# Which rows of the wq gradient go out in which transfer: five three-way splits become two two-way splits, and the last group's stores become whole

## The chip, the cores and the metric

The kernel runs on one core of one Trainium2 chip. The metric is device time in microseconds of one execution; the time before is the median of three, 730.28 us (729.32 to 732.16). The profile is one execution of the same program, taken by the hardware profiler. Engines are named as the profile names them: PE (matrix multiply), DVE (vector), ACT (scalar), POOL (GpSimd) and SP (SyncE, which here only starts transfers). Transfers move on 16 DMA engines which all queues share; the profile gives their mean busy share, and the packet records of the trace give every packet's start, duration, size and queue, but not the number of the DMA engine it ran on.

## The reference: what is computed

One decode token (x of 640 values, bfloat16) goes through a layer norm; beside the residual there are two branches, attention over a cache of 8192 keys for 32 heads of 128, and a gated MLP of width 1728. The kernel returns the forward output and the gradients of all inputs but the MLP's unused one:

```python
xn = _layernorm(x, axis=-1)
return x + _A_ref(xn, A_k_cache, A_v_cache, A_wq, A_wo) + _B_ref(xn, B_w1, B_w3, B_w2)
...
_out, _vjp = jax.vjp(_f, A_x, A_k_cache, A_v_cache, A_wq, A_wo, B_w1, B_w3, B_w2)
_grads = _vjp(grad_out)
```

For the time two things matter. Each of the 32 heads reads its keys and values (2 MB each) once, and writes a gradient of the same size for each: 4 times 2 MB in and out per head. And the gradients of wq (640 by 4096) and wo (4096 by 640) are outer products, 5.2 MB each, written over the weights in SBUF and stored from there.

## The kernel before, in words

**Heads.** `head(h)` (L745) transposes K and V of one head on PE, forms scores, softmax and the backward pass, and `outer` (L464) writes the gradients over K and V in place on DVE. `store` (L477) sends a gradient out and calls `load_next` (L122), which loads the next K or V into a freed slot; there are ten slots of 2 MB, and `lag` keeps at least three of them free before the next load goes out. All of these transfers go through `fifo` (L104), that is through SP's queue, in the order V store, load, K store, load. Every one has 128 rows (partitions) of 16 KB.

**Groups.** Four heads make a group, g from 0 to 7. `load_group` (L109) brings 512 columns of wq as a tile of 128 rows by 5 by 512 (`wq_g`, 640 KB: five pieces of 1 KB in each row) and the matching rows of wo (`wo_g`, 640 KB: four pieces of 1,280 bytes in each row). Three buffers of each rotate. After a group's heads, during the next group, `fin_wo(g)` (L517) overwrites `wo_g` with its gradient and `fin_wq(g, ci)` (L523), called for ci from 0 to 4 at five places of the heads (L683 to L714), does the same to `wq_g`; both end in `store_group` (L505). After the last piece of wq, `fin_wq` also loads group g + 3 on POOL's queue.

**What `store_group` does before.** `fin_wq` calls it with `split` true for groups 1 to 5. Then the tile goes out in three transfers: rows 0 to 4 and rows 5 to 125 on POOL's queue, rows 126 and 127 on SP's. The wo gradients, and wq of groups 0 and 6, go out whole on POOL's queue. Group 7 is finished after all heads (L835 to L839), and each of its two gradients goes out in two transfers on SP's queue, rows 0 to 59 and rows 60 to 127.

**The end.** After group 7, DVE, PE and ACT form the two short rows (L841 to L867); ACT starts four small stores of them (L849, L867). SP and ACT take the semaphores of their transfers from one ring of eight in turn, so a transfer waits until the one eight places earlier in that ring has landed, besides its own data.

Of the kernel before, what the change touches and what calls it, by code (L numbers as in the profile page):

```python
# [16 lines left out]
P = 128  # L17
# [4 lines left out]
def kernel(  # L22
# [32 lines left out]
    NG = H // GH  # L55
    GW = GH * DH
# [23 lines left out]
    dwq_v = out_4.rearrange("(ci p) n -> p ci n", p=P)  # L80
# [23 lines left out]
    def fifo(out_, in_):  # L104
        nc.sync.dma_start(out_, in_)
# [3 lines left out]
    def load_group(g, eng):  # L109
        wq_g = wpool.tile([P, NC, GW], BF16, name="wq_g", tag="wq_g")  # L110
        eng.dma_start(wq_g[:], wq_v[:, :, g * GW:(g + 1) * GW])
        wo_g = wpool.tile([P, GH, D], BF16, name="wo_g", tag="wo_g")
        eng.dma_start(wo_g[:], wo_v[:, g * GH:(g + 1) * GH, :])
        grp[g] = dict(wq=wq_g, wo=wo_g)
# [389 lines left out]

    def store_group(g, dst, t, split=False):  # L505
        if split:
            for lo, hi in ((0, 5), (5, 126)):
                nc.gpsimd.dma_start(dst[lo:hi], t[lo:hi])
            fifo(dst[126:P], t[126:P])
            return  # L510
        if g < NG - 1:
            nc.gpsimd.dma_start(dst, t[:])
            return
        for lo, hi in ((0, 60), (60, P)):
            fifo(dst[lo:hi], t[lo:hi])

    def fin_wo(g):  # L517
        G_ = grp[g]
        for hh in range(GH):
            nc.vector.tensor_scalar(G_["wo"][:, hh, :], g_bc[:], G_["od"][:, hh, 0:1], None, ALU.mult)  # L520
        store_group(g, dwo_v[:, g * GH:(g + 1) * GH, :], G_["wo"])

    def fin_wq(g, ci):  # L523
        G_ = grp[g]
        wq_g, dqb = G_["wq"], G_["dqb"]
        nc.vector.scalar_tensor_tensor(wq_g[:, ci, :], wq_g[:, ci, :], 1.0, dqb, ALU.mult, ALU.mult,  # L526
                                       accum_out=dxa[:, ci, g:g + 1])
        nc.vector.tensor_scalar(wq_g[:, ci, :], dqb, xn_col[:, ci:ci + 1], None, ALU.mult)
        if ci == NC - 1:
            store_group(g, dwq_v[:, :, g * GW:(g + 1) * GW], wq_g, 1 <= g <= 5)  # L530
            grp.pop(g)
            if g + 3 < NG:
                load_group(g + 3, nc.gpsimd)
# [149 lines left out]
    def side_k(h):  # L683
        g, hh = divmod(h, GH)
        if hh == 1 and g > 0:
            fin_wq(g - 1, 0)
        elif hh == 2 and g > 0:
            fin_wq(g - 1, 3)
        elif hh == 3 and g + 1 < NG:
            prep_do(g + 1, 1)  # L690

    def side_m(h):
        g, hh = divmod(h, GH)
        if hh == 0 and g > 0:
            fin_od(g - 1)
        elif hh == 1 and g > 0:
            fin_wq(g - 1, 1)
        elif hh == 2 and g > 0:
            fin_wq(g - 1, 4)
        elif hh == 3 and g + 1 < NG:  # L700
            prep_do(g + 1, 2)
            prep_do(g + 1, 3)
# [195 lines left out]
```

## Time and profile before

| What | Value |
|---|---|
| median of three runs | 730.28 us (729.32, 730.28, 732.16) |
| profiled execution | span 727.5 us from the first to the last instruction; its time with what lies around the span is not given apart |
| PE, DVE, ACT, POOL busy | 83%, 63%, 52%, 4% of the span |
| read from and written to HBM | 151.34 MB each, 416 GB/s over the span |
| transfers on SP's queue (q1) | 22578 packets, 277.75 MB, 90.5% of 16 engines |
| transfers on POOL's queue (q0) | 5968 packets, 24.94 MB, 8.5% of 16 engines |

How to read it: the page cuts the span into 40 slices and gives busy shares in tenths; the row "DMA" is the mean over the 16 DMA engines. The table by stage gives the same share for any stretch. The list of SP's waits tells what ended each wait ahead of a transfer's start. A transfer's landing is counted by a semaphore that rises once for each DMA engine that took part, so the trace holds up to 16 landing times for each transfer, the first being the DMA engine that was furthest ahead and the last the one furthest behind.

### The profile page before, as it was taken

How to read it: one execution, taken by the hardware profiler on the slowest of the kernel's cores; microseconds unless marked ns; L12 is line 12 of the kernel's file. 1: busy time of each engine (PE TensorE's matmuls, PEld its weight loads, DVE VectorE, ACT ScalarE, POOL GpSimd, SP SyncE). 2: the span in 40 equal slices, each digit the busy share in tenths (PEclk: the TensorE clock that was granted, in tenths of full speed). 3: DMA queues.
4: the chain of work that ended last, by engine and by line, in shares of the span. 5: the costliest groups of instructions: out<-in, count | busy, mean ns of one | idle time of the engine just before them, and what ended most of it. 6: DMA issues, size and time to landing. Idle time of an engine off the chain costs nothing.

```text
span 727.5 us, 12942 instructions
## 1 busy us (share of the span) xinstructions
PE 603.3 (83%) x5186; PEld 377.1 (52%) x5193; DVE 459.8 (63%) x811; ACT 376.2 (52%) x727; POOL 32.3 (4%) x48
## 2 busy tenths in 40 slices
PE   4989489999899989888897789878796988988930
PEld 2547366665565556555454456445554555545510
DVE  4169646688868776667565756457665666667581
ACT  3640746665666566545454546455463555655510
POOL 0010100000000000000010000000000000000000
PEclk9997799999999999989998989899998999999965
DMA  9999999999999999999999999999999999999995
GB/s 351 400 411 421 428 426 430 427 426 430 420 420 431 430 412 420 426 428 421 420 425 428 430 426 428 420 431 428 421 422 427 429 425 423 425 432 427 426 415 221
DMA packets 28625, 303.54 MB, mean 417 GB/s; under 512 B 3354, under 2 KB 5929, under 8 KB 11924
## 3 DMA queue, kind: packets, MB, share of 16 engines
q1 hardware_dynamic: 22578, 277.75, 90.5%
q0 software_dynamic: 5968, 24.94, 8.5%
q8 instruction: 41, 0.67, 0.4%
q14 instruction: 20, 0.16, 0.1%
q10 hardware_dynamic: 18, 0.01, 0.0%
HBM read 151.34 MB, written 151.34 MB: 416 GB/s over the span
## 4 chain that ended last, share of the span: by engine, by line
DMA 51%; PE 36%; DVE 7%; ACT 2%; issue 1%; SPq 0%; ACTq 0%; DVEq 0%
DMA kv<-in_A_v_cache_dram 20%; PE pT L318 17%; DMA out_dram<-kv 16%; DMA kv<-in_A_k_cache_dram 14%; PE sA L339 5%; PE dA L339 4%; PE X L433 3%; DVE kv L466 3%; PE m L356 2%; DMA wo_g<-in_A_wo_dram 2%; ACT KT L320 1%; PE gu_ps L561 1%; PE pT L266 1%; PE m L400 1%; ACT KT L346 0%
## 5 line engine op out<-in xcount | busy, mean ns | idle before, releaser
L320 ACT COPY KT<-pT 128x512 f32<-128x512 f32 x512 | 288.3, 588 | 227.9 <-PE pT L318 208.6
L318 PE MATMUL pT<-ident_f,kv 128*128 128x128 f32 x2048 | 308.2, 290 | 53.7 <-DMA kv<-in_A_v_cache_dram 24.2
L318 PEld LDWEIGHTS pT<-ident_f,kv 128*128 128x128 f32 x2048 | 237.4, 149 | 146.2 <-PE pT L318 51.8
L466 DVE TENSOR_TENSOR kv<-qd,U 128x4096 bf16<-128x4096 bf16 x64 | 146.0, 2284 | 0.0
L466 DVE TENSOR_TENSOR kv<-qd,P 128x4096 bf16<-128x4096 bf16 x64 | 143.6, 2285 | 0.0
L433 PE MATMUL X<-kv,Z 128*32 128x512 bf16 x1024 | 97.1, 413 | 1.8 <-DVE Z L450 1.8
L339 PE MATMUL dA<-KT,qz 128*32 128x512 bf16 x512 | 84.2, 408 | 0.0
L339 PE MATMUL sA<-KT,qz 128*32 128x512 bf16 x512 | 83.5, 406 | 0.0
L416 DVE SCALAR_TENSOR_TENSOR U<-m,P 128x64 bf16<-128x64 f32 x32 | 7.5, 233 | 87.4 <-PE m L356 87.4
L433 PEld LDWEIGHTS <-Z 128*32 128x32 bf16 x1024 | 33.2, 101 | 35.3 <-issue 8.7
L339 PEld LDWEIGHTS <-qz 128*32 128x32 bf16 x1024 | 29.5, 95 | 40.8 <-issue 38.3
L382 DVE TENSOR_REDUCE mrow<-m 128x1 f32<-128x64 f32 x32 | 7.1, 223 | 68.4 <-PE m L356 68.3
L356 PE MATMUL m<-selc,KT 64*128 64x64 f32 x256 | 30.5, 242 | 10.3 <-ACT KT L346 10.3
L356 PEld LDWEIGHTS m<-selc,KT 64*128 64x128 f32 x256 | 21.5, 144 | 33.2 <-ACT KT L346 22.1
L376 ACT CAST qd<-pT 128x256 bf16<-128x256 f32 x32 | 11.9, 372 | 39.9 <-DVE kv L466 28.7
L389 DVE TENSOR_REDUCE negM<-m 128x1 f32<-128x128 f32 x32 | 9.3, 292 | 33.0 <-PE m L386 33.0
L526 DVE SCALAR_TENSOR_TENSOR wq_g<-wq_g,side 128x512 bf16<-128x512 bf16 x40 | 27.3, 683 | 0.0
L257 DVE SCALAR_TENSOR_TENSOR side<-wo_g,g_bc 128x640 bf16<-128x640 bf16 x32 | 26.2, 819 | 1.3 <-DMA wo_g<-in_A_wo_dram 0.9
L448 DVE SCALAR_TENSOR_TENSOR U<-m,P 128x128 bf16<-128x128 f32 x32 | 11.4, 356 | 16.3 <-PE m L446 16.3
L406 DVE RECIPROCAL rZ<-m 128x1 f32<-128x1 f32 x32 | 5.3, 166 | 24.2 <-PE m L400 24.2
L346 ACT COPY KT<-dA 64x512 f32<-64x512 f32 x32 | 18.6, 582 | 3.7 <-PE dA L339 3.7
L346 ACT COPY KT<-sA 64x512 f32<-64x512 f32 x32 | 18.6, 581 | 2.1 <-PE sA L339 1.9
(162 smaller groups left out, 372.7 us busy)
## 6 DMA issues: line engine op xcount, KB each, us to landing
out_dram<-kv SPq DMA_DIRECT2D x64, 2048.0 KB
kv<-in_A_k_cache_dram SPq DMA_DIRECT2D x32, 2048.0 KB
kv<-in_A_v_cache_dram SPq DMA_DIRECT2D x32, 2048.0 KB
wq_g<-in_A_wq_dram POOLq DMA_DIRECT2D x7, 640.0 KB, 13.4
wo_g<-in_A_wo_dram POOLq DMA_DIRECT2D x7, 640.0 KB, 19.1
out_dram<-wo_g POOLq DMA_DIRECT2D x7, 640.0 KB, 14.4
kv<-in_B_w_dram SPq DMA_DIRECT2D x2, 1728.0 KB
out_dram<-kv POOLq DMA_DIRECT2D x2, 1728.0 KB, 23.5
```

The source lines that it names most:

```text
L257: nc.vector.scalar_tensor_tensor(junk[:], G_["wo"][:, hh, :], 1.0, g_bc[:], ALU.mult, ALU.mult, accum_out=G_["do"][:, hh:hh + 1])
L318: nc.tensor.transpose(pT[:, k * P:(k + 1) * P], W3[:, 4 * c + k, :], ident_f[:])
L320: nc.scalar.copy(KT[:].rearrange("p k w -> p (k w)"), pT[:])
L339: nc.tensor.matmul(S_[kind][q:q + QW, :], lhsT=S_["qz"][:, o:o + QW], rhs=KTb[c][:, par, :], start=(c0 == 0 and par == 0), stop=(c0 == NCH ...
L346: nc.scalar.copy(XS[0:QH].rearrange("p k w -> p (k w)"), S_.pop(kind)[0:QH, :])
L356: nc.tensor.matmul(S_["m"][:, b0:b0 + 4 * J].rearrange("p (x c k t) -> p k x c t", x=4, k=4, t=2)[:, k], lhsT=XS[0:QH, k, :], rhs=selc[0:Q ...
L376: nc.scalar.copy(qd[:].rearrange("p a d -> p (a d)"), hd[h].pop("ps_r"))
L389: nc.vector.tensor_reduce(S_["negM"][:], S_["m"][:, 2 * J:2 * J + P], AX.X, ALU.max, negate=True)
L433: nc.tensor.matmul(xg["X"][q:q + QW, :], lhsT=Z[:, o:o + QW], rhs=W[:, N4 * i:N4 * (i + 1)], start=(slot == 0 and i < 4), stop=(slot == NS ...
L448: nc.vector.scalar_tensor_tensor(S_["U2"][:], S_["V"][:, 0:J].unsqueeze(2).to_broadcast([P, J, 2]), S_["m"][:, OC + NS:OC + NS + 1], S_["P ...
L466: nc.vector.tensor_tensor(dst[:, lo * DH:hi * DH].rearrange("p (j a b) -> p j a b", a=DH // 2, b=2), vec.rearrange("p (a b) -> p a b", b=2 ...
L526: nc.vector.scalar_tensor_tensor(wq_g[:, ci, :], wq_g[:, ci, :], 1.0, dqb, ALU.mult, ALU.mult, accum_out=dxa[:, ci, g:g + 1])
```

## The change

`store_group` loses its three-way split. For groups 2 and 4 the wq gradient goes out in two transfers on POOL's queue, rows 0 to 118 and rows 119 to 127. For groups 1, 3 and 5 it goes out whole on POOL's queue. The two gradients of group 7 each go out whole on SP's queue. Nothing is computed differently.

```diff
     def store_group(g, dst, t, split=False):
         if split:
-            for lo, hi in ((0, 5), (5, 126)):
+            for lo, hi in ((0, 119), (119, P)):
                 nc.gpsimd.dma_start(dst[lo:hi], t[lo:hi])
-            fifo(dst[126:P], t[126:P])
-            return
-        if g < NG - 1:
+        elif g < NG - 1:
             nc.gpsimd.dma_start(dst, t[:])
-            return
-        for lo, hi in ((0, 60), (60, P)):
-            fifo(dst[lo:hi], t[lo:hi])
+        else:
+            fifo(dst, t[:])
...
         if ci == NC - 1:
-            store_group(g, dwq_v[:, :, g * GW:(g + 1) * GW], wq_g, 1 <= g <= 5)
+            store_group(g, dwq_v[:, :, g * GW:(g + 1) * GW], wq_g, g in (2, 4))
```

In the instruction order of the changed kernel SP has 139 transfers where it had 146, and POOL 37 where it had 40; PE, DVE and ACT do the same work in the same order. With five transfers fewer ahead of it, each later transfer of SP takes another semaphore of the ring. The whole wo store of group 7 waits, besides its data, for the V store of head 30, as the 60-row one did. The whole wq store waits for the first of ACT's small stores of L849.

## The prediction

> **What bounds the kernel now.** I read the page's slices first, then the table by stage, SP's waits, and last the landing times and packet records of the trace.
>
> ```profile
> PE   4989489999899989888897789878796988988930
> DMA  9999999999999999999999999999999999999995
> ```
>
> PE has gaps in every part of the run; the DMA engines have none until the last slice. The table by stage (columns: stretch, its length, PE, PEld, DVE, ACT, POOL busy, granted clock, DMA share, GB/s) says so in numbers, and shows where it ends:
>
> ```profile
> 250.00:690.00 440.00, 379.16 (x3173) 233.22 (x3178) 276.78 (x455) 236.70 (x471) 19.56 (x24) 0.93 1.01 425
> 700.00:710.00 10.00, 1.81 (x12) 0.88 (x12) 8.71 (x23) 0.59 (x1) 0.00 (x0) 0.50 0.97 415
> 710.00:720.00 10.00, 0.93 (x3) 0.59 (x3) 2.24 (x12) 0.00 (x0) 0.00 (x0) 0.50 0.81 304
> 720.00:727.50 7.50, 0.00 (x0) 0.00 (x0) 0.00 (x0) 0.00 (x0) 0.00 (x0) 0.50 0.26 92
> ```
>
> From 250 to 690 us all 16 DMA engines are busy without a gap (1.01: records overlap by some ns). After 710 they run out one after the other: 0.19 x 10 + 0.74 x 7.5 = 7.5 us of the mean engine are lost. So the time is **the work of the DMA engine that has most of it**. The bytes don't change; what the change can move is who carries them. With perfect balance 7.5 us could be won; that is the bound on that side.
>
> The last DMA engine is also kept waiting by a start that comes late:
>
> ```profile
> L105 SPq DMA_DIRECT2D out_dram<-wq_g x7: 257/523/2915, 261.2 to 721.1; - x7
> SPq L105 <- DMA out_dram<-fin_bf: 5.4, 1, 5.4
> ```
>
> The first row (least/median/most ns, first and last start) ends with the 68-row wq store, started at 721.1. SP's waits say for what: ACT's first 4-row store, whose semaphore it shares. It landed at 721.07 and the 68 rows at 726.59, 0.9 us before the span's end.
>
> **Who carries what.** The 2 MB store of K of head 31, started at 704.28, has 16 landing times: 710.44, 710.45, 710.47, 710.75, 711.39, 712.32, then 715.80, 717.69, 717.95, 718.59, 719.05, 719.10, 719.59, 720.98, 721.60, 723.58. Six DMA engines are early, ten late. At 250 us the same list was 5.9 us wide, and it widens at each of the five split stores; the splits make most of that width. The packet sizes on POOL's queue show how: per split there are 11 packets of 3,072 bytes with 143 of 4,096 (11 engines with 55 KB, so 11 rows each), and 5 of 1,024 with 5 of 4,096 (five engines with one row each). The largest divisor of 121 up to 16 is 11, that of 5 is 5, together 16. The other side's share of each transfer is filled with packets of 4 to 16 bytes that take 6 or 7 ns. Likewise the 60 rows have 15 landings of data, the 68 rows four, the two rows two.
>
> I then followed each DMA engine through the records (its next packet starts 3 to 4 ns before the recorded end of its last), from a quiet moment before each split to one behind it. In all five, the two engines that take SP's two rows are among the five with one row: **the same five each time**. Four of the five run ahead. The fifth, call it X, is about nine packets behind the next of them all the way: counted at nine packets for a 2 MB transfer it stands at 510 against 519 to 521 at 289 us, and at 1140 against 1150 to 1161 at 640 us. It was the last of all 16 before the first split. It can't be one of the four with 68 rows: those landed by 720.89, so they had finished K of head 31 by about 716.5. By its place in the order, ninth of 16, X's landing above is 717.95, or the next, 718.59.
>
> **The price of a row.** Steps from one packet's start to the next, from the records: 155 ns for 4,096 bytes, 118 for 3,072, 43 for 1,024 (42 on SP's queue), 52 for 1,280, 607 for 16,384. Per engine and group:
> - whole: 10 x 155 + 6 = 1.56 us
> - before, five-row side: 155 + 43 + 6, with the other transfer's filling 0.10 = 0.31 us
> - before, 121-row side: 13 x 155 + 118 + 6, filling 0.02 = 2.16 us
> - after: 119 = 7 x 17, so seven engines take 17 rows: 21 x 155 + 43 + 6 + 0.02 = 3.32 us; nine take one row of the 9: 0.20 + 0.16 = 0.36 us.
>
> **The change part by part.**
> 1. Groups 1, 3, 5 whole, 2 and 4 in 119 + 9. Sum of five groups for the seven: 3 x 1.56 + 2 x 3.32 = 11.3 us; for the nine: 3 x 1.56 + 2 x 0.36 = 5.4 us. Before: 5 x 0.31 = 1.5 us on the five, 5 x 2.16 = 10.8 us on the eleven. Which engines are the seven? The trace before has no such transfer. Its nearest row is that the first of two split transfers always begins at the same engines, the five; the first is now the 119 rows. So I take the five as part of the seven. X then gets 11.3 - 1.5 = **+9.8 us**; if it were one of the nine, +3.9 us. The two that lose SP's two rows (5 x 0.22 = 1.1 us) get +8.7; the other two of the seven +0.5; the nine 5.4 - 10.8 = **-5.4 us**.
> 2. Five 2-row stores leave SP. Each cost it 0.3 to 2.9 us of issue; that is hidden, since the engines have several transfers queued (the store of V of head 30, started at 682.29, landed last at 709.07), so 0; without the queue it would be 5 us at most over the run. POOL's next loads no longer wait for those two rows (108 us of its waits in four pieces, the longest 34). The group loaded then is first read four heads later, 78 us by the starts of two such stores (251.6 and 329.3), so that too is 0; without that cover 34 us less on POOL would count.
> 3. POOL issues one transfer in place of two (0.88 against 1.63 us) in three groups; POOL is busy 4%: 0.
> 4. Group 7 whole: each engine carries 32 x 52 + 40 x 42 ns + two counts = 3.4 us behind its last 2 MB, where the four carried 8.8 and the late ten 1.7. The wq store no longer waits for the 4-row store; it waits for ACT's first small store, which landed at 712.13, and its own data were ready at 710.3. So it starts by about 713, ahead of every late engine's turn. The stall of 8 us goes. What is late next is the engine with most work.
>
> **The sum.** X: 717.95 + 9.8 + 3.4 = 731.1 us (731.8 from the other landing), where the last landing was 726.6; plus 0.9 to the end of the span: 732.0 to 732.7, I take 732.3. That is +4.8 us on the profile's 727.5. The median is 2.8 us above that span, so **735.0 us**, 0.65% slower. 0.5% (3.65 us) is about what a measurement of this kernel can tell from no change.
>
> **A rule weighed.** The packet counts above say that a POOL transfer uses as many engines as divide its rows. The Trainium skill, "DMA: Bandwidth & Descriptors", section "Why a DMA increments its semaphore by 16 and not by 1", states the same rule, and a round-robin cursor that picks them; but it adds that some POOL transfers use all 16 engines whatever the rows, with at most eight of 127 rows on each. By that exception the 121 rows would show no 3,072-byte packet at all, so the row speaks against it here. Under it X would get only 8 or 9 rows of each split, and the end would be near rival C's. The same page, section "Latency and other measured facts", says that engines 7 and 15 are usually slower than others. If the cursor starts at engine 0 both would be among the nine, which speaks for the change. By it the engine last at 723.58 could be one of them and lose 5.4 us, which leaves the sum for X as it is. No record here numbers the engines; the one that takes none of the 60 rows landed K of head 31 at 710.75, among the six early ones.
>
> **Rivals.**
> - **B, X isn't last.** X's handicap belongs to something in this program's start, not to the engine, or I followed the wrong one. Then the last is at worst the late engine at 723.58, if it is one of the two others of the seven: 723.58 + 0.5 + 3.4 + 0.9 = 728.4, measured 731.2, +0.1%. For it: ten late engines, two places. Against: X in the same place in five stretches.
> - **C, the split doesn't do what its numbers say**: the 119 rows are spread like a whole tile, eight on an engine. X gets 3 x 1.56 + 2 x (1.56 + 0.20) - 1.5 = 6.7 us and ends at 717.95 + 6.7 + 3.4 + 0.9 = 728.9, measured 731.7, +0.2%. For it: the 60 rows did reach 15 engines. Against: the packet counts of the 121.
> - **D, the other side: not slower.** The nine begin where the five did, so X is one of them and the early engines fill up. X ends at 717.95 + 3.9 + 3.4 + 0.9 = 726.1, measured 728.9, -0.2%. The point that decides: X makes the kernel slower only from 727.5 - 0.9 - 3.4 - 717.95 = 5.2 us of added work; 3.9 is under it, 9.8 over. For it: the trace before has no transfer of seven engines to go by. Against: the first transfer of a split began at the same five each time. Over 0.5% faster it is only if all engines end by 723.8 of the span; the bound is -7.5 us.
>
> **How the numbers follow.** Forecast 0.57; B 0.23; C 0.07; D 0.13. The predicted time is the forecast's, the likeliest. Its own spread, X's landing up to 719.6 and an execution 1.5 us off either way, gives 733.2 to 738; nine in ten of that lies over 733.9, so 0.51, and 0.01 from B and C: 0.52 slower by over 0.5%. A third of D and a little of B, where even the late engine is relieved, make 0.08 faster. The rest, 0.40, is within. The range runs from 728.0, just under D, to 738.0; about 0.15 lie outside.
>
> **What would show it.** Right: the landings of the last K store are no longer six early and ten late; one straggler lands near 728, alone, and the last stage of the table shows a DMA share still lower than 0.26. Packets of POOL's queue: per split 21 of 4,096 and one of 1,024 on seven engines, and no 3,072. SP's last start falls from 721 to about 713. Wrong: a last landing under 725, or more than one engine at the end.

## The result, and the profile after

The changed kernel takes **735.79 us** (median of six, 735.55 to 737.55) against 730.4 us before in the same session (728.42 to 732.16): a ratio of 1.0079, 95% interval [1.0062, 1.0096] (it isn't formed from the two medians, which give 1.0074). The forecast was 735.0, slower by 0.65%. The profiled execution has a span of 734.2 us and took 735.95.

From the page after, PE and the mean of the DMA engines in 40 slices:

```profile
PE   4989589999899999797887898787897888877830
DMA  9999999999999999999999999999999999999982
```

Before, the DMA row was 9 in every slice but the last, a 5; now the last two slices are 8 and 2. In what follows, "engine" means DMA engine unless it is named. The table by stage after (stretch, its length, PE, PEld, DVE, ACT, POOL busy, granted clock, DMA share, GB/s) gives it in us:

```profile
250.00:690.00 440.00, 370.06 (x3127) 227.49 (x3131) 277.77 (x451) 231.89 (x461) 17.69 (x21) 0.95 1.01 426
690.00:700.00 10.00, 10.00 (x76) 5.80 (x74) 3.36 (x6) 6.01 (x12) 0.00 (x0) 0.83 0.84 360
700.00:710.00 10.00, 2.85 (x29) 1.82 (x27) 9.31 (x8) 0.75 (x2) 0.00 (x0) 0.70 0.91 379
710.00:720.00 10.00, 2.38 (x14) 1.39 (x14) 7.85 (x31) 0.59 (x1) 0.00 (x0) 0.50 0.85 351
720.00:727.50 7.50, 0.37 (x1) 0.08 (x1) 0.60 (x3) 0.00 (x0) 0.00 (x0) 0.50 0.32 116
727.50:734.20 6.70, 0.00 (x0) 0.00 (x0) 0.00 (x0) 0.00 (x0) 0.00 (x0) 0.50 0.05 17
```

Up to 690 us nothing has changed: 426 GB/s against 425, no gap on any engine. The last row is the result: for 6.7 us the DMA share is 0.05, which is one engine of 16 (1/16 = 0.06), while no compute engine of the core works. New is also that engines run dry in the middle: 0.84 and 0.91 from 690 to 710, where before had 0.97 from 700 to 710, and in the stretch ahead of it 0.99:

```profile
690.00:700.00 10.00, 5.13 (x55) 2.64 (x54) 9.27 (x10) 1.92 (x5) 0.00 (x0) 0.85 0.99 419
```

The chain that ended last shows how one late engine reaches the others (start and length in us, before and then after):

```profile
657.53 25.79 DMA kv<-in_A_v_cache_dram
683.46 1.06 PE pT L318 x8
```

```profile
662.90 26.42 DMA kv<-in_A_v_cache_dram
689.45 1.10 PE pT L318 x8
```

This is the load of V of head 31. After, fifteen engines have landed it by 680.2 and the sixteenth at 689.3 (before, the last was at 683.3). PE starts on it only then, so the work that feeds the last stores of all engines comes 6 us later.

The landings say the same engine by engine. The 2 MB store of K of head 31, started at 710.31 (before 704.28), lands on 15 engines between 716.98 and 720.11, and on the sixteenth at **729.65**, alone. The two stores behind it end the same way: wo at 731.22, 9.5 us behind the next engine, wq at 732.86, 9.4 us behind it.

The wq stores and the SP waits after (first fence: the tile's issues, least/median/most ns, first and last start; second: what an SP wait ended with, total us, how many, the longest):

```profile
L508 POOL DMA_DIRECT2D out_dram<-wq_g x4: 588/955/1314, 329.6 to 503.9; - x4
L105 SPq DMA_DIRECT2D out_dram<-wq_g x1: 382/382/382, 719.7 to 719.7; - x1
```

```profile
SPq L890 <- DMA out_dram<-wq_g: 12.7, 1, 12.7
SPq L105 <- DMA out_dram<-KT: 4.3, 1, 4.3
```

The wait for ACT's 4-row store (`fin_bf`, 5.4 us before) is gone, and a wait for ACT's first small store (`KT`) is in its place, as the prediction had it. SP's last transfer starts at 719.7, however, not by about 713. Its last wait, for that transfer to land, takes 12.7 us.

### The profile page after: what moved, and what is told of

The parts are those of the page before. It is cut to its first block, busy times and chain, and to the rows that moved or that the text cites. A ratio compares the mean times of both kernels' runs of the same rounds, so it can differ in the third digit from the quotient of the medians.

```text
span 734.2 us, 12906 instructions
## 1 busy us (share of the span) xinstructions
PE 601.6 (82%) x5186; PEld 376.4 (51%) x5193; DVE 461.6 (63%) x811; ACT 376.0 (51%) x727; POOL 30.4 (4%) x45
## 3 DMA queue, kind: packets, MB, share of 16 engines
q0 software_dynamic: 5888, 24.99, 8.4%
## 4 chain that ended last, share of the span: by engine, by line
DMA 56%; PE 32%; DVE 6%; ACT 2%; issue 1%; SPq 0%; ACTq 0%; DVEq 0%
DMA out_dram<-kv 22%; DMA kv<-in_A_v_cache_dram 18%; PE pT L318 15%; DMA kv<-in_A_k_cache_dram 15%; PE sA L339 4%; PE dA L339 3%; PE X L433 3%; DVE kv L466 3%; PE m L356 2%; DMA wo_g<-in_A_wo_dram 2%; ACT KT L320 1%; PE gu_ps L558 1%; PE dh_ps L569 1%; ACT KT L346 1%; PE acc L199 1%
```

## The experiments

The theory: the time is that of the DMA engine with most work; this is X, the fifth engine from the one at which the first transfer of a split begins; the change gives it 17 rows of two groups and eight of three, where it had one of each. The rivals: the whole stores of the last group make the loss; any engine that gets 17 rows would become the straggler; the number or the oddness of the transfers costs by itself.

Times are medians, ratios are to the kernel before on the same chip with their 95% intervals (experiments 1 to 4 ran on one chip, 5 to 8 on a second, 9 and 10 on a third, 11 and 12 on a fourth); the landings are those of K's store of head 31 in the profiled execution, whose own time stands beside them. In every run the time is the span plus 1.8 us.

| Program | Median us | Ratio | First, 15th and last landing | Profiled execution |
|---|---|---|---|---|
| before | 730.28 (three runs) | 1 | 710.4, 721.6, 723.6 | 729.3 (span + 1.8) |
| changed | 735.79 | 1.0079 [1.0062, 1.0096] | 717.0, 720.1, 729.6 | 735.95 |
| changed, order swapped | 729.87 | 0.9997 [0.9984, 1.0010] | 710.5, 721.8, 723.9 | 730.19 |
| before, last group whole | 729.15 | 0.9993 [0.9979, 1.0008] | 714.6, 724.8, 727.2 | 733.26 |
| changed, last group in 60 and 68 | 735.08 | 1.0072 [1.0054, 1.0091] | 716.6, 721.6, 730.1 | 734.76 |
| everything whole | 732.60 | 1.0034 [1.0020, 1.0047] | 712.4, 721.0, 725.8 | 732.11 |
| fifth engine spared | 727.06 | 0.9953 [0.9939, 0.9968] | 709.3, 718.8, 720.5 | 726.80 |
| fourth engine spared | 733.15 | 1.0034 [1.0021, 1.0047] | 713.3, 721.1, 726.7 | 733.04 |
| changed, start moved by seven | 730.90 | 1.0011 [1.0001, 1.0021] | 711.5, 723.2, 724.6 | 731.07 |
| changed, four groups split | 740.15 | 1.0140 [1.0119, 1.0160] | 723.2, 726.2, 735.8 | 742.20 |
| fifth spared in seven groups | 728.70 | 0.9981 [0.9967, 0.9995] | 711.7, 721.8, 723.4 | 729.77 |
| swapped, four groups split | 734.90 | 1.0061 [1.0043, 1.0079] | 715.5, 726.6, 726.8 | 733.22 |
| fifth spared, once more | 726.40 | 0.9944 [0.9930, 0.9958] | 710.2, 719.7, 720.0 | 726.51 |
| fifth spared in six groups | 727.41 | 0.9952 [0.9938, 0.9965] | 711.3, 720.8, 722.5 | 728.91 |

**1. The same bytes, engines exchanged.** Against the changed kernel:

```diff
-            for lo, hi in ((0, 119), (119, P)):
+            for lo, hi in ((0, 9), (9, P)):
```

> The two split groups go out as 9 rows and then 119 rows instead of 119 and then 9: the same bytes, the same number of transfers, the same sizes of packet; only which engines take 17 rows and which take one is exchanged. My theory (the time is X's, and X is the fifth engine from the one at which the first transfer of a split begins): X is now among the nine with one row, so it has 2 x (3.32 - 0.36) = 5.9 us less than in the changed kernel, where it landed K of head 31 at 729.65: 723.7. With the final stores of 3.2 us and 1.3 us to the end of the span that is a span of 728 (726 to 729), measured 729.5 to 731, 0.7 to 0.9% under the changed kernel. The landings of K of head 31 show no engine 9 us behind the rest. Rival 1 (the loss comes from the whole stores of the last group, or from the number of transfers, not from the engine that got the rows): the time stays at 735 to 736 and one engine is still some 9 us behind. Rival 2 (any engine that gets 17 rows twice becomes the straggler): one engine again lands alone, near 729, time 735 to 736.

Measured 729.87: the whole loss is gone, with the same rows, sizes and number of transfers. The table by stage of the swapped program:

```profile
710.00:720.00 10.00, 0.93 (x3) 0.59 (x3) 2.39 (x14) 0.00 (x0) 0.00 (x0) 0.50 0.71 288
720.00:728.40 8.40, 0.00 (x0) 0.00 (x0) 0.00 (x0) 0.00 (x0) 0.00 (x0) 0.50 0.18 68
```

From 720 us some three engines (0.18 x 16) run on the mean instead of one at the end. The last landing is 723.89, where 723.7 was worked out. Both rivals fall: neither the number of transfers nor 17 rows on some engine costs 5 us; it matters on which engine they lie.

**2. Only the last group whole.** Against before:

```diff
-        for lo, hi in ((0, 60), (60, P)):
-            fifo(dst[lo:hi], t[lo:hi])
+        fifo(dst, t[:])
```

> The kernel before with one part of the change: the two gradients of group 7 leave whole, the five three-way splits stay. My theory: the end is set by before's late engines (last landing of K of head 31 at 723.58), which now carry 3.4 us instead of 1.7 or 8.8 behind it: 723.6 + 3.4 + 0.9 = 727.9, at most 728.5, so the span moves by +0.4 to +1 us and the time reads 730 to 731.5, the same as before. SP's last start falls from 721 to 713 to 716, as the stall for the four-row store goes. Rival (the whole final stores make the loss): +4 to +5 us, 734 to 736.

Measured 729.15, the same as before. The rival asked for 734 to 736. Its profiled execution is the slowest of its twelve, 4 us over the median, so its landings aren't set beside the others; SP's last start in it, 717.3, is later than the 713 to 716 expected. The stall that the change removes is worth nothing that can be measured.

**3. Only the middle splits.** Against the changed kernel the last group goes out in rows 0 to 59 and 60 to 127 again:

```diff
-            fifo(dst, t[:])
+            for lo, hi in ((0, 60), (60, P)):
+                fifo(dst[lo:hi], t[lo:hi])
```

> The changed kernel with the last group's gradients still in 60 and 68 rows: only the middle splits are changed. My theory: X carries the middle rows as in the changed kernel; of the last group it carries what one of fifteen or of eleven engines carries, four rows of each gradient (1.7 us) instead of eight (3.4 us), so the end comes 1.7 us earlier than in the changed kernel: measured 733.5 to 734.5, +0.45 to +0.6% on the kernel before. One engine lands K of head 31 at 728.5 to 730, alone. Rival (the final stores make the loss): as before, 730 to 731.

Measured 735.08, so nearly all of the loss lies in the middle splits. That was 0.6 us above the expectation, and the two intervals overlap, so what the last group adds isn't measured. In the profiled execution X does carry less behind K's store, 1.6 us (730.09 to 731.68) against 3.2, but began 0.4 us later.

**4. No split at all.** Against the changed kernel:

```diff
-            store_group(g, dwq_v[:, :, g * GW:(g + 1) * GW], wq_g, g in (2, 4))
+            store_group(g, dwq_v[:, :, g * GW:(g + 1) * GW], wq_g, False)
```

> Every wq gradient leaves whole: no split anywhere, and the last group whole too. My theory (one engine, X, lags by itself and equal shares leave it there): X has 2 x (3.32 - 1.56) = 3.5 us less than in the changed kernel, 729.65 - 3.5 = 726.1 for K of head 31, or from the kernel before 717.95 + 5 x (1.56 - 0.31) = 724.2; with 3.2 and 1.3 us that is a span of 728.7 to 730.6, measured 731 to 733. The fifteen others land within 3 us of each other some 6 to 8 us ahead of X. Rival (the lag of X comes from the rows that it is given, not from the engine): all sixteen land within 3 us and the time is 725 to 727, faster than both kernels.

Measured 732.6, between the two as expected. With equal rows on every engine one still lands alone, at 725.77, 4.7 us behind the next: the lag isn't made by the rows that X is given. One part of the expectation was wrong: the fifteen others aren't within 3 us, they spread over 8.7.

**5 and 6. Spare one engine, then its neighbour.** The splits of groups 1 to 5 become three transfers whose divisors (for group 1: 5 rows on 5 engines, 120 on 15, 3 on 3) leave two rows on the fifth engine from the start and eight or nine on each other; the last group is whole. Against before:

```diff
-            for lo, hi in ((0, 5), (5, 126)):
+            m1, m2 = {1: (5, 125), 2: (14, 119), 3: (8, 113), 4: (2, 122), 5: (11, 116)}[g]
+            for lo, hi in ((0, m1), (m1, m2), (m2, P)):
                 nc.gpsimd.dma_start(dst[lo:hi], t[lo:hi])
-            fifo(dst[126:P], t[126:P])
-            return
...
```

The second program has every cut one row earlier (4 and 124, 13 and 118, 7 and 112, 1 and 121, 10 and 115), which spares the fourth engine.

> The wq gradients of groups 1 to 5 leave in three transfers on POOL's queue, cut so that by the rule of divisors and the turning start one engine, the fifth from the start, takes two rows of each group and the fifteen others eight or nine; the last group leaves whole. My theory: that engine is X. With every gradient whole X landed K of head 31 at 725.8; 5 x 6 rows fewer at 0.195 us are 5.9 us, with fillings 0.2 back: 720.1. The next late engine, at 721.0 there, gets two or three rows more (0.5): 721.5 is now the end of that store, plus 3.2 and 1.3 us: a span of 726, measured 727 to 728.5, 0.2 to 0.4% under the kernel before, and no engine lands alone. Rival 1 (X is another engine): X gets two or three rows more than in the program with whole stores, 732.6 to 733.5. Rival 2 (15 rows more of small transfers on POOL and the odd row counts cost by themselves): 731 or more with all engines together.

> As the run that spares the fifth engine from the start, but cut so that its neighbour, the fourth, is spared. My theory: X isn't spared and carries the two or three rows more of the others: 725.8 + 0.4 + 3.2 + 1.3 = 730.7 of the span, measured 732.5 to 733.5, 4 to 5.5 us over the run that spares the fifth. One engine lands alone, 4 to 5 us behind the next. Rival (any relief of one engine helps, or X is the fourth): 727 to 729.

Measured 727.06 and 733.15: 6.1 us between two programs that differ by one row in each cut. The rows by stage, first of the one that spares the fifth, then of the one that spares the fourth:

```profile
710.00:720.00 10.00, 0.62 (x3) 0.25 (x2) 1.12 (x5) 0.00 (x0) 0.00 (x0) 0.50 0.72 286
720.00:725.00 5.00, 0.00 (x0) 0.00 (x0) 0.00 (x0) 0.00 (x0) 0.00 (x0) 0.50 0.08 29
```

```profile
710.00:720.00 10.00, 0.93 (x3) 0.59 (x3) 5.17 (x21) 0.00 (x0) 0.00 (x0) 0.50 0.84 337
720.00:731.30 11.30, 0.00 (x0) 0.00 (x0) 0.00 (x0) 0.00 (x0) 0.00 (x0) 0.50 0.11 42
```

With the fifth spared, all engines land K by 720.50 (720.1 worked out for X); with the fourth spared, one engine lands alone at 726.73, 5.6 us behind the next. So X is one engine, and it is the fifth. The first of the two programs is faster than both kernels.

**7. Move the start, not the split.** Against the changed kernel:

```diff
-            for lo, hi in ((0, 119), (119, P)):
+            cuts = ((0, 96), (96, 114), (114, P)) if g == 0 else ((0, 119), (119, P))
+            for lo, hi in cuts:
...
-            store_group(g, dwq_v[:, :, g * GW:(g + 1) * GW], wq_g, g in (2, 4))
+            store_group(g, dwq_v[:, :, g * GW:(g + 1) * GW], wq_g, g in (0, 2, 4))
```

> The changed kernel with its two splits (119 rows, then 9) as they are; only the wq store of group 0, early in the run, is cut in 96, 18 and 14 rows: 16, 9 and 14 engines by the rule, 39 in all, so the start for all that follows on POOL's queue moves on by seven engines, and each engine has still seven, eight or nine rows of that store. My theory: the seven engines that take 17 rows are now the eighth to the fourteenth and X, the fifth, takes one row: 729.65 - 5.9 + 0.2 = 724.0 for K of head 31, span 728.5, measured 729.5 to 731, like the swapped order. Rival (the start of a split is fixed, or the order of 119 and 9 is what matters): 735 to 737 with one engine 9 us behind.

Measured 730.90. The 119 rows still leave first, and 4.9 us of the loss are gone because an earlier transfer used 39 engine places instead of 16. Its wq issues on POOL:

```profile
L509 POOL DMA_DIRECT2D out_dram<-wq_g x7: 588/652/1302, 180.1 to 501.9; - x7
```

Three of the seven are group 0's at 180 us; the other four are the changed kernel's, and they meet other engines. X doesn't move with the start.

**8. Twice the dose.** Against the changed kernel:

```diff
-            store_group(g, dwq_v[:, :, g * GW:(g + 1) * GW], wq_g, g in (2, 4))
+            store_group(g, dwq_v[:, :, g * GW:(g + 1) * GW], wq_g, g in (1, 2, 4, 5))
```

> The changed kernel with four groups (1, 2, 4, 5) split in 119 and 9 rows instead of two. My theory (a price for each row on X): two more splits at 3.32 - 1.56 = 1.76 us: X lands K of head 31 at 729.65 + 3.5 = 733.2, time 738.8 to 740, 3.0 to 4.0 us over the changed kernel. Rival (the loss of a split is paid once, or the engines that run behind are given less of the later transfers): 737 or less.

Measured 740.15. By the medians no split, two and four give 732.60, 735.79 and 740.15 (on three chips): 1.6 us a split and then 2.2, where 1.76 was worked out; the four groups together are 7.55 us, 1.9 each. The stage rows show one engine (0.05) for the last 10.4 us:

```profile
720.00:730.00 10.00, 0.92 (x3) 0.58 (x3) 5.87 (x24) 0.00 (x0) 0.00 (x0) 0.50 0.68 265
730.00:740.40 10.40, 0.00 (x0) 0.00 (x0) 0.00 (x0) 0.00 (x0) 0.00 (x0) 0.50 0.05 20
```

**9. Spare the fifth in more groups.** Against the program that spares the fifth engine, the cuts are used in groups 0 to 6 (`[g % 5]` in a list of the five pairs, `g < NG - 1`).

> The cuts that spare the fifth engine, now in all seven wq gradients of groups 0 to 6 instead of five: two groups more at 6 rows fewer, 12 x 0.195 = 2.3 us less on X. With five groups X was still the last by a little (720.5 for K of head 31, the next 718.75). My theory: X drops to 718.2 and the next engine, at 718.75 plus 0.1 to 0.4, is the end: 719.0, so 1.5 us less than with five groups: measured 725 to 726, 0.6 to 0.7% under the kernel before, and from here on sparing X brings nothing more. Rival (X isn't the last any more with five groups, the whole end is set by all engines together): 727, no change from five groups.

A miss: 728.70, 1.6 us over the program with five groups, not under it. The stretch from 100 to 220 us, of the program with five groups and then of the one with seven:

```profile
100.00:220.00 120.00, 115.64 (x1016) 72.03 (x1017) 79.37 (x133) 76.09 (x154) 3.29 (x4) 0.99 1.01 425
```

```profile
100.00:220.00 120.00, 115.96 (x1020) 73.40 (x1017) 77.81 (x132) 75.41 (x152) 5.36 (x8) 0.97 1.00 415
```

In its profiled execution (729.77, the slowest of its twelve) 10 GB/s are missing for 120 us, 120 x 10 / 425 = 2.8 us on all engines. Most of that lies at 120 to 150 us (five groups, then seven):

```profile
120.00:150.00 30.00, 29.08 (x262) 18.29 (x262) 20.59 (x37) 20.07 (x42) 0.62 (x1) 1.00 1.01 426
```

```profile
120.00:150.00 30.00, 29.46 (x263) 18.59 (x251) 21.44 (x33) 19.51 (x40) 0.00 (x0) 1.00 1.00 400
```

That is 30 x 26 / 426 = 1.8 of the 2.8 us, and it is ahead of the first transfer that differs (the wq store at about 180), so it isn't the cut's.

**10. Give the 17 rows to the seven others, twice as often.** Against the swapped program, groups 1, 2, 4 and 5 are split.

> The swapped order, 9 rows and then 119, in four groups (1, 2, 4, 5) instead of two. My theory (the time is that of the engine with most work, whichever it is): X falls by 2 x (1.56 - 0.36) = 2.4 us to 721.5 for K of head 31, but the latest of the seven that now take 17 rows four times rises by 2 x 1.76 = 3.5 us, from 721.8 to 725.3, and takes X's place: 725.3 + 3.2 + 1.3 = 729.8, measured 730.5 to 732.5, 0.6 to 2.6 us over the swapped order with two groups, where X's relief alone would give 727.5. Rival (only X ever sets the time): 727 to 728.

Measured 734.90: another engine does take over. The end is no longer one straggler; seven engines land K between 722.9 and 726.8, nine by 717.2, and after 720 us the stage row has a third of the engines busy:

```profile
720.00:731.50 11.50, 0.00 (x0) 0.00 (x0) 0.00 (x0) 0.00 (x0) 0.00 (x0) 0.50 0.34 133
```

The size was underrated by 2.4 us or more (profiled execution: 1.5, by 726.8 against 725.3); where the rest of the median comes from wasn't found.

**11 and 12. Five groups once more, and six.** The first is the program that spares the fifth engine, unchanged; the second uses its cuts in groups 1 to 6.

> The program that spares the fifth engine in groups 1 to 5 once more, on one chip beside the program below. If its first result was the program's and not that chip's, 726.5 to 728, 0.3 to 0.6% under the kernel before. If sparing X in five groups and in seven are the same and the first result was an accident of the chip, 728.5 to 729.

> The cuts that spare the fifth engine in groups 1 to 6; group 0, whose cut came with 1.6 us more instead of 1.5 less, leaves whole again. If the cut of group 0 did the harm (an early stretch in which loads and stores are slowed), X at 720.5 - 1.2 = 719.3 and the next engine at 718.8 to 719.2 give 0 to 1.2 us under five groups: 726 to 727. If five groups are already enough and every further cut only costs, 727.5 to 729.

Measured 726.40 and 727.41; the first result was the program's. The intervals overlap: a sixth group brings nothing that can be seen. That seven groups are slower than six (728.70 on another chip) points to group 0's cut, but wasn't separated from the early stretch above.

**Which engine is last, and why.** The 16 engines can be followed through the packet records in stretches in which POOL's queue is silent, with each transfer's landings as a check. On fifteen engines the step from one 16 KB packet to the next is 607 ns for loads and stores alike, but for single longer ones. On one it is 626 to 639 ns in stores, in the mean of a stretch, and 608 to 612 in loads. There is such an engine in all fourteen traces. In the changed kernel (480 to 506, 605 to 640 and 650 to 677 us; 634 to 636 ns) this is the engine furthest behind in all three stretches; likewise late in the run with everything whole, with the fourth spared and in the swapped program. In before it is the eighth from behind at 663 us, where engines that took 11 rows have passed it to the rear. With the fifth spared in five groups it is still the last in the first execution (641 to 667 us) and the fourth from behind in the second (643 to 669); in seven groups it is the fifth from behind. So with five groups X has just about caught up with the others, and further cuts have little to win.

Eight store packets of a 2 MB store at 28 ns more are 0.22 us; 64 stores make 14.3 us. With equal rows the distance from the first to the last landing in fact grows from 1.7 us at 42 us to 15.2 us at 684. X is slow only while the others run: at the end of the changed kernel, where it runs alone from 723.7 us on, its store packets step at 607 ns too.

## Why the prediction was right

- **What bounds the kernel.** Right. Up to 690 us the rows are the same, and the spans follow the last landing of K's store, by 4.3 to 4.7 us in every program whose last group is whole.
- **X, and that the change puts it on the side of 17 rows.** Right, and the step that carried the forecast. It was taken from the nearest row (the first transfer of a split begins at the same five), and the exchange of 119 and 9, the moved start and the two spared engines each confirm it.
- **What X's handicap is.** The text had X "about nine packets behind the next of them all the way". That holds against the nearest of its four peers only. Its own counts hold the rest: against the fastest peer it was 11 packets behind at 289 us (510 against 521) and 21 at 640 (1140 against 1161). The handicap grows with every store.
- **X's landing before, 717.95 or 718.59.** Misread. The ninth place is right at 663 us, but a handicap that grows goes on pushing X back. Its slow stores land some 0.5 us behind their last packet, those of the other engines about 0.35; followed by both, X is ninth at 662.74, tenth at 672.62 and 689.31, eleventh at 699.41. So it landed K of head 31 at 719.05 or 719.10, and the sum began 1.1 us too early.
- **+9.8 us on X.** 10.6 from there (729.65 against 719.05). The two splits have their price (1.6 to 1.9 us each by the medians, 1.76 worked out). The step from one row to eight is 6.7 us (725.77 with everything whole, against 719.05), where 5 x 1.25 = 6.3 was worked out. Two executions of one kernel differ by more than is left, so the price of a row may be right.
- **Behind the last 2 MB, 3.4 us.** Measured 3.2.
- **0.9 us to the end of the span.** Measured 1.3.
- **2.8 us from span to median.** The weak step. 1.8 us of it lie around the span in every run; the other 1.0 was only that before's profiled execution (727.5 + 1.8 = 729.3, the lowest of its three) was a fast one. The changed kernel's is 0.2 us over its median. The span was forecast at 732.3 and measured at 734.2; the 1.9 us too few there (1.1 in X's landing before, 0.8 in its rows) and the 1.2 too many here leave 0.8 in the time. That the time was met within 0.8 us is in part luck: without the second error it would have been 2.
- **The wq store of the last group.** The wait was named rightly, the start was not: 719.7 instead of about 713. The step took ACT's first small store to land at 712.13 as before; it landed at 719.64. X also lands the last loads later, and the whole tail slid with them (K's store from 704.28 to 710.31). It cost nothing, since X's queue was full until 729.65.
- **Fewer stores on SP, one transfer less on POOL: 0.** Right, as far as 2 us in 730 can show it.
- **The packets.** Per split 21 of 4,096 and one of 1,024 on seven engines, one and one on nine, and none of 3,072: the row of the queue has them in sum.

```profile
q0 software_dynamic: 5888, 24.99, 8.4%
```

  Of the 5,888 packets 2,232 have 4,096 bytes and 32 have 1,024: 1,920 of the whole tiles and 2 x (7 x 21 + 9) = 312; 2 x (7 + 9) = 32. Rival C (eight rows on an engine) falls with it.
- **The signs.** One straggler near 728: 729.65, alone. Last stage under 0.26: 0.05, but 0.32 in the stretch from 720 to 727.5, since the tail had slid. SP's last start at 713: no.
- **The rivals.** B (X isn't last) falls: X is the last by 9.5 us. D (the nine begin where the five did) was worked out at 728.9; the swapped order makes it true, at 729.87.
- **The rule weighed.** The divisor's rule held in the packet counts, and the turning start in the program that moves it. The Trainium skill, "DMA: Bandwidth & Descriptors", section "Latency and other measured facts", has engines 7 and 15 as the slower ones. No record here numbers the engines; the runs show one slow engine, not two. By the same page's rule that a transfer from SP takes the lowest-numbered engines (section "Why a DMA increments its semaphore by 16 and not by 1"), SP's two rows lie on 0 and 1, both among the five, so their last, X, is one of 1 to 4. By the same rule the 68 rows lie on 0 to 3, and X isn't one of these (with 60 and 68 rows behind the changed splits they landed wo by 724.40, when X had not landed K), so X would be 4; that is an estimate from the page's rule.

## What to carry to other kernels

Where the DMA engines are full, look at the landings one by one, not at the mean share: the time is one engine's, and a partition count without the divisor 16 decides which engines get the rows. Exchange the parts of a split as a test: the same bytes in the other order made 5.9 us of difference here. Equal shares aren't the best when one engine is slow by itself: two rows on it and eight or nine on the others took 0.5% off the kernel before, where eleven engines with 11 rows were late, and 0.8% off equal shares (0.9953 against 1.0034).

## What the runs showed of the hardware

- One of the 16 DMA engines steps at 626 to 639 ns through the 16 KB packets of stores where the others step at 607, on each of four chips. It is the fifth in POOL's order wherever the runs tell. Alone at the end of the changed kernel it steps at 607 too. Why it is slow beside the others, no run shows.
- The same engines carry a queue that the page calls "instruction" (packets, MB, share of 16 engines):

```profile
q8 instruction: 41, 0.67, 0.4%
```

  41 packets of 16 KB, one about every 17 us, on changing engines; each takes 0.9 to 1.1 us, and the data packet behind it another 0.4 to 0.6 over its 607 ns: some 1.4 us of lag for that engine. They may be what spreads the other fifteen with everything whole; no run shows it.
- A POOL transfer's rows go to as many engines as the largest divisor up to 16 (119 rows: seven engines with 21 packets of 4,096 each). The runs fit a ring on which the next such transfer begins where the last ended: 39 places taken early moved two splits 150 and 320 us later, by 4.9 us of time.
